# Four buffers instead of two for the expert weights, with the scratch of the dynamic DMAs halved

## The chip, the cores and the metric

The kernel runs on one core of a Trainium2 chip. The time is that of the device, in microseconds (us), from one run of the whole program; lower is better. Three runs of the kernel before gave 1428.39, 1423.75 and 1426.98 us, with a median of 1426.98 us.

## What is computed

Three stages follow each other. An attention between a sequence and a small state gives 8 x 544 = 4352 rows of 512 values. Each row is then sent to the one of eight experts whose embedding is nearest, and goes through that expert's two matrices (512 x 1024 and 1024 x 512). At last all rows go through a dense two-layer network (512 x 2048 and 2048 x 512). Cut to what matters, the reference is this:

```python
# attention, for x (8,8,512,64) and state (8,8,32,64)
a  = softmax(x @ state.T / 8);   xread = a  @ state
a2 = softmax(state @ x.T / 8);   sread = a2 @ x
x = concatenate([xread, sread], axis=2)          # then 4352 rows of 512
# experts
logits = normalise(x) @ normalise(expert_emb).T / tau
expert_idx = argmax(logits, axis=1)
gate_w = softmax(logits)[arange(N), expert_idx]
for e in range(8):
    mask = expert_idx == e
    h = maximum(x[mask] @ w1[e], 0.0)
    out[mask] = gate_w[mask, None] * (h @ w2[e])
# dense network
h = out @ w_in
g = h * clip(h + 3.0, 0.0, 6.0) / 6.0
result = g @ w_out
```

## The kernel before

**Stages.** The attention writes its rows to a table in DRAM (`xd`). The rows are sorted by expert into slots of 128 rows. The first five slots belong to the largest expert and form the lead: four of them are worked on together (`QUAD`) and one beside them (`FIFTH`), with the same weights. Behind them come 11 units of two slots and ten units of one slot (`RUN`); a few more units stand in branches at the end, for other distributions of the rows. The finished rows of a slot are stored to a second table in DRAM (`ysd`). The dense network takes blocks of 256 rows from that table, 17 of them (`Y`, `F1`, `F2`), and its matmuls are interleaved with those of the expert units as soon as the rows are there.

**Products in three parts.** Every matrix is split into a high part in the fp32r format and a low part, which is the rest. A product is three matmuls: high by high, low by high and high by low.

**The weights of an expert.** `load_w` (line 1236) loads 512 KB, 128 partitions x 2 x 512 values, into a buffer called `raw`, by a DMA that SP issues: line 1244 for the first matrix and line 1247 for the second. One unit takes four loads of each, and all units together take 176. A load is two pieces of 128 x 512 values. For each piece the high part `wh` is written by ACT or DVE (line 1258) and the low part `wl` by DVE or POOL (line 1261); the `raw` buffer is free again when both of its pieces have been split. The tiles `wh` and `wl` come from a pool of `NW = 3` pieces, and a piece is free when TensorE has used it. The first matrix is multiplied in `L1w` (line 1420, result `h_ps`), the second in `L2` (line 1523, result `y_ps`).

**The dense weights.** The dense matrices are 64-bit in DRAM. `Conv` (lines 267 to 326) loads them in 512 KB parts through ACT's queue, rebuilds the 32-bit values in several operations of ACT and DVE, and splits them into `wih`, `wil`, `woh` and `wol`. This takes place while the lead and the first units run.

**The rows of the dense network.** `Y` (line 1576) loads the rows of a block (`yl`, line 1590) through SP's queue, behind the stores to `ysd`. DVE transposes them, and ACT and DVE split them into `yh` and `yw`. `F1` (line 1629, result `u_ps`) and `F2` (line 1664, result `o`) are the matmuls.

**The order of the work.** Nothing is scheduled on the chip: each engine runs its instructions in the order in which the program emits them. That order comes from a planner in the kernel, the class `Sched`. Every piece of work has a cost on each engine that may do it, a due time, dependencies and buffers. The planner keeps one `Ring` for each kind of buffer, with the times at which its buffers come free. It then picks again and again the work with the smallest sum of possible start and weighted due time, so the sizes of the rings shape the order of all queues. The line that makes the rings is

```python
    NRAW, NW, NROW, NGX = 2, 3, 5, 4
    RG = {n: Ring(k) for n, k in dict(... raw=NRAW, w=NW, wraw=NRAW, ...).items()}
```

and the pool of the real buffers is opened with the same number, when the attention's memory has been given back:

```python
        pools(mctx, (("raw", dict(bufs=NRAW)), ("wp", dict(bufs=NW)), ...
```

**Memory.** The scratch at the bottom of the on-chip memory holds the descriptors of the DMAs that POOL issues (the gathers `xg` and `xq` from `xd`, the stores to `ysd` and the scattered stores of the result). By default it takes 16 KB of each partition. The constants and the dense weights lie above it, then the pools named above, `raw` first.

Of the kernel before, what the change touches and what calls it, by code (L numbers as in the profile page):

```python
# [154 lines left out]
def kernel(  # L155
# [12 lines left out]
    nc = tc.nc  # L168
# [74 lines left out]
    copy = {"A": ACT.copy, "D": DVE.tensor_copy}  # L243


    NRAW, NW, NROW, NGX = 2, 3, 5, 4
    NAX, NXT, NSC, NE2, NE1, NA2, NAH, NXR = (3, 3, 1, 1, 2, 1, 1, 1)
    NHX = 4
    RG = {n: Ring(k) for n, k in dict(
# [1633 lines left out]
```

## Time and profile before

| | |
|---|---|
| median of three runs | 1426.98 us (1423.75 to 1428.39) |
| the profiled execution's own time | 1424.93 us |
| its span | 1423.3 us |
| matmuls on TensorE (PE) busy | 1337.1 us, 94% of the span |
| VectorE (DVE) busy | 871.8 us, 61% |
| ScalarE (ACT) busy | 608.6 us, 43% |
| GpSimd (POOL) busy | 410.6 us, 29% |
| mean granted TensorE clock | 0.961 of full speed |

The span is what the hardware profiler saw of the program's instructions; the execution's own time is 1.6 us longer. PE is TensorE's matmuls, PEld its weight loads, SP the engine that only issues DMAs; a q behind a name (SPq, ACTq, POOLq) is the queue of that engine. A wait is written in square brackets: idle time before an instruction, and what ended it. A granted clock of 0.5 is 1.2 GHz and one of 1.0 is 2.4 GHz.

### The profile page before, as it was taken

The numbers are of one execution on the slowest core, as the hardware profiler recorded it, in microseconds if no ns is written. First come the engines' busy times: TensorE is split into PE (matmuls) and PEld (weight loads), VectorE is DVE, ScalarE is ACT, GpSimd is POOL, SyncE is SP. The second block draws the span as 40 slices with busy tenths as digits, with TensorE's granted clock in tenths as the row PEclk, the third lists the DMA queues.
The fourth block names the chain that finished last, engine by engine and source line by source line (L and its number), as shares of the span: only waits on it lengthen the run. The fifth ranks groups of instructions, "written<-read, shape, count | busy, mean of one in ns | idle before, by whom it ended". The sixth has DMA issues, their size and how long they took to land. (4 is left out here: it accounts for less than half of the span.)

```text
span 1423.3 us, 25424 instructions
## 1 busy us (share of the span) xinstructions
PE 1337.1 (94%) x9176; PEld 1189.1 (84%) x9176; DVE 871.8 (61%) x2047; ACT 608.6 (43%) x1318; POOL 410.6 (29%) x430
## 2 busy tenths in 40 slices
PE   7885797988899999999999999999999999999997
PEld 5664676877789889888989899998989999899996
DVE  5777966787566464656555446677776776334432
ACT  4885536676434333332424333343444443323332
POOL 3332545523432232233214223333223211100000
PEclk8996788989999999999999999999999999999999
DMA  7654347566563332333333233455454544101000
GB/s 175 182 167 168 107 135 195 172 192 204 153 190 97 112 99 97 113 104 106 112 100 118 90 105 124 163 154 165 150 164 149 164 141 151 46 15 30 16 16 16
DMA packets 151828, 176.48 MB, mean 124 GB/s; under 512 B 43856, under 2 KB 116560, under 8 KB 150672
## 3 DMA queue, kind: packets, MB, share of 16 engines
q1 hardware_dynamic: 128608, 121.47, 27.8%
q0 software_dynamic: 12336, 36.55, 8.1%
q10 hardware_dynamic: 10752, 16.78, 3.7%
q8 instruction: 73, 1.20, 0.4%
q14 instruction: 59, 0.48, 0.1%
HBM read 146.65 MB, written 28.10 MB: 123 GB/s over the span
## 5 line engine op out<-in xcount | busy, mean ns | idle before, releaser
L1629 PE MATMUL u_ps<-yh,wih 128*128 128x256 f32 x1088 | 308.3, 283 | 4.8 <-ACT yh L1605 3.7
L1629 PE MATMUL u_ps<-yw,wih 128*128 128x256 f32 x1088 | 308.2, 283 | 0.3 <-DVE yw L1608 0.3
L1629 PE MATMUL u_ps<-yh,wil 128*128 128x256 f32 x1088 | 307.9, 283 | 0.0
L1633 ACT ACTIVATE r<-u_ps,three 128x256 f32<-128x256 f32 x272 | 129.3, 475 | 356.7 <-PE u_ps L1629 337.2
L1636 DVE SCALAR_TENSOR_TENSOR u_ps<-r,u_ps 128x256 f32<-128x256 f32 x272 | 116.4, 428 | 232.3 <-ACT r L1633 219.7
L1629 PEld LDWEIGHTS u_ps<-yh,wih 128*128 128x128 f32 x1088 | 206.9, 190 | 14.3 <-ACT yh L1605 3.9
L1664 PE MATMUL o<-woh,gh 128*128 128x512 f32 x544 | 216.2, 397 | 0.8 <-DVE yo L1678 0.6
L1664 PE MATMUL o<-wol,gh 128*128 128x512 f32 x544 | 215.9, 397 | 0.0
L1664 PE MATMUL o<-woh,gl 128*128 128x512 f32 x544 | 215.1, 395 | 0.0
L1629 PEld LDWEIGHTS u_ps<-yw,wih 128*128 128x128 f32 x1088 | 206.8, 190 | 9.0 <-DVE yw L1608 0.5
L1629 PEld LDWEIGHTS u_ps<-yh,wil 128*128 128x128 f32 x1088 | 207.6, 191 | 0.0
L1261 DVE TENSOR_TENSOR wl<-raw,wh 128x512 fp32r<-128x512 f32 x280 | 195.8, 709 | 7.1 <-ACT wh L1258 2.3
L1640 ACT CAST gh<-u_ps 128x256 fp32r<-128x256 f32 x272 | 101.5, 373 | 206.7 <-PE o L1664 170.6
L1643 DVE TENSOR_TENSOR gl<-u_ps,gh 128x256 fp32r<-128x256 f32 x272 | 115.0, 423 | 114.3 <-ACT gh L1640 104.1
L1523 PE MATMUL y_ps<-wh,hx 128*128 128x512 f32 x512 | 184.9, 398 | 0.0
L1261 POOL TENSOR_TENSOR wl<-raw,wh 128x512 fp32r<-128x512 f32 x72 | 101.8, 1415 | 232.8 <-DVE wh L1258 125.7
L1289 POOL DMA_INDIRECT xq<-xd,qidx x128 | 130.9, 1023 | 59.0 <-issue 32.3
L1420 PE MATMUL h_ps<-xt,wh 128*128 128x256 f32 x704 | 141.0, 289 | 0.0
L1258 DVE CAST wh<-raw 128x512 fp32r<-128x512 f32 x226 | 101.2, 450 | 51.1 <-PE y_ps L1523 20.5
L1683 POOL DMA_INDIRECT out_dram<-yo,ix x34 | 38.0, 1118 | 301.4 <-DVE yo L1678 203.1
L1664 PEld LDWEIGHTS o<-woh,gl 128*128 128x128 f32 x544 | 102.4, 188 | 24.2
L1420 PE MATMUL h_ps<-xt,wl 128*128 128x256 f32 x352 | 103.0, 293 | 17.8 <-DVE wl L1261 11.9
(297 smaller groups left out, 2230.4 us busy)
## 6 DMA issues: line engine op xcount, KB each, us to landing
raw<-in_moe_w_dram SPq DMA_DIRECT2D x176, 512.0 KB
xd<-xr SPq DMA_DIRECT2D x8, 1088.0 KB
yl<-ysd SPq DMA_DIRECT2D x136, 64.0 KB
ysd<-yt POOLq DMA_DIRECT2D x32, 256.5 KB
xb<-in_x_dram SPq DMA_DIRECT2D x48, 128.0 KB
yw<-in_moe_w_out_dram ACTq DMA_DIRECT2D x9, 512.0 KB
cv_raw<-in_moe_w_in_dram ACTq DMA_DIRECT2D x8, 512.0 KB
yh<-in_moe_w_in_dram ACTq DMA_DIRECT2D x8, 512.0 KB
```

What stands on the lines that cost most here:

```text
L1258: copy[e](pc["hi"], box["t"][:, j, :])
L1261: eng[e].tensor_tensor(pc["lo"], box["t"][:, j, :], f32(pc["hi"]), op=ALU.subtract)
L1289: POOL.indirect_dma_start(q[:, j * QW:(j + 1) * QW], None, xd_q, index(qidx[:, j, s:s + 1]))
L1420: PE.matmul(out(f), pc[w][:, (2 * c + f) * 128:(2 * c + f + 1) * 128], u.xt[a][:, 2 * j + c, 256 * hf:256 * hf + 256], start=new and c == ...
L1523: PE.matmul(u.y[i], u.ht[t][:, a, lo + 128 * i:lo + 128 * i + 128], pc[w], start=c == 0 and k == 0, stop=c == KF - 1 and k == 2)
L1629: PE.matmul(p, w, y[:, k, :], start=k == 0 and j == 0, stop=k == KD - 1 and j == 2)
L1633: ACT.activation(q["r"], q["p"], AF.Relu, bias=pool["three"][:, 0:1], scale=unit_i)
L1636: DVE.scalar_tensor_tensor(q["p"], q["r"], 6.0, q["p"], op0=ALU.min, op1=ALU.mult)
L1640: ACT.copy(q["h"], q["p"])
L1643: DVE.tensor_tensor(q["l"], q["p"], f32(q["h"]), op=ALU.subtract)
L1664: PE.matmul(o["o"][a], g[:, a * 128:(a + 1) * 128], w, start=m == 0 and j == 0, stop=m == KFF - 1 and j == 2)
L1683: POOL.indirect_dma_start(out, bass.IndirectOffsetOnAxis(ap=o["ix"][:, a:a + 1], axis=0), box["t"], None)
```

## The change

The number of `raw` buffers goes from two to four, in the pool and in the planner's rings `raw` and `wraw` alike. Each buffer takes 4 KB of a partition, so 8 KB more are needed. The scratch of the dynamic DMAs is made 8 KB instead of 16 KB. The pools from `wp` upwards therefore keep their addresses, and what lies below `raw` moves down by 8 KB.

```diff
-    NRAW, NW, NROW, NGX = 2, 3, 5, 4
+    NRAW, NW, NROW, NGX = 4, 3, 5, 4
...
-    nc = _bacc.Bacc("TRN2", target_bir_lowering=False, num_devices=1)
+    nc = _bacc.Bacc("TRN2", target_bir_lowering=False, num_devices=1,
+                    dynamic_dma_scratch_size=8192)
```

## Rows read from the trace of the kernel before

**Rows 1.** The page: busy time of each engine, and the chain's shares.
```profile
PE 1337.1 (94%) x9176; PEld 1189.1 (84%) x9176; DVE 871.8 (61%) x2047; ACT 608.6 (43%) x1318; POOL 410.6 (29%) x430
...
PE 14%; DMA 0%; POOLq 0%; issue 0%; ACT 0%
```

**Rows 2.** Busy times of two stretches: PE, PEld, DVE, ACT, POOL, granted clock, DMA share, GB/s.
```profile
200.00:400.00 200.00, 172.55 (x967) 151.17 (x967) 143.21 (x327) 114.38 (x237) 86.72 (x83) 0.91 0.60 184
400.00:1220.00 820.00, 819.18 (x5223) 739.10 (x5223) 508.60 (x1172) 318.54 (x729) 240.40 (x233) 1.00 0.41 127
```

**Rows 3.** Waits of PE from 200 to 400 us: total, times, longest.
```profile
PE h_ps L1420 <- DVE wl L1261: 11.9, 7, 5.4
...
PE y_ps L1523 <- DVE wl L1261: 5.6, 4, 2.4
PE u_ps L1629 <- ACT yh L1605: 3.7, 1, 3.7
```

**Rows 4.** Waits for and by the loads, 137 to 420 us: SP, DVE, ACT.
```profile
SPq L1247 <- DVE wl L1261: 83.6, 16, 15.4
...
DVE wh L1258 <- DMA raw<-in_moe_w_dram: 1.9, 3, 0.9
...
ACT wh L1258 <- DMA raw<-in_moe_w_dram: 4.0, 4, 1.8
```

**Rows 5.** Timeline of SP's queue: start, duration, instruction, count.
```profile
213.94 9.96 SPq L1244 DMA_DIRECT2D raw<-in_moe_w_dram  x2
...
228.48 0.40 SPq L1244 DMA_DIRECT2D raw<-in_moe_w_dram  x1
...
235.92 6.72 SPq L1590 DMA_DIRECT2D yl<-ysd  x8
242.91 0.41 SPq L1244 DMA_DIRECT2D raw<-in_moe_w_dram  x1
```

**Rows 6.** Timeline of PE and ACT around the first dense block.
```profile
247.02 0.38 PE L1629 MATMUL u_ps<-yh,wih 128*128 128x256 f32 x1 [3.69 <-ACT yh L1605]
...
248.00 1.64 ACT L1258 CAST wh<-raw 128x512 fp32r<-128x512 f32 x3
...
253.06 0.39 PE L1420 MATMUL h_ps<-xt,wl 128*128 128x256 f32 x1 [0.76 <-DVE wl L1261]
```

**Rows 7.** Busy times of shorter stretches, columns as in rows 2.
```profile
137.00:147.00 10.00, 2.27 (x24) 1.78 (x22) 8.17 (x30) 4.04 (x8) 6.80 (x7) 0.50 0.77 259
...
236.00:243.00 7.00, 7.00 (x43) 7.00 (x43) 2.16 (x4) 1.81 (x3) 2.49 (x3) 0.66 1.08 250
...
247.00:253.00 6.00, 4.94 (x25) 4.53 (x25) 5.96 (x7) 3.74 (x7) 4.74 (x4) 0.72 0.25 76
...
300.00:345.00 45.00, 36.35 (x198) 31.68 (x199) 39.95 (x85) 33.62 (x65) 9.90 (x9) 0.89 0.62 206
```

**Rows 8.** The chain that ended last: one of its pieces.
```profile
1224.85 1.44 PE u_ps L1629 x12
```

**Rows 9.** Timeline of a later gap: load, split, matmul.
```profile
289.94 1.72 SPq L1244 DMA_DIRECT2D raw<-in_moe_w_dram  x2
...
302.82 0.68 DVE L1261 TENSOR_TENSOR wl<-raw,wh 128x512 fp32r<-128x512 f32 x1
...
303.56 0.58 PE L1420 MATMUL h_ps<-xt,wl 128*128 128x256 f32 x1 [3.64 <-DVE wl L1261]
```

**Rows 10.** Timeline of the longest gap.
```profile
386.93 0.56 POOL L1554 DMA_DIRECT2D ysd<-yt  x1 [5.12 <-DMA ysd<-yt]
...
389.71 0.58 PE L1420 MATMUL h_ps<-xt,wl 128*128 128x256 f32 x1 [5.42 <-DVE wl L1261]
```

**Rows 11.** Timeline of the lead's start.
```profile
151.59 1.97 PE L1314 MATMUL m_g<-ident,xp 128*128 128x128 f32 x8 [1.20 <-ACT xp L1309]
...
156.89 1.28 DVE L1320 TENSOR_TENSOR x<-m_g,x 128x512 fp32r<-128x512 f32 x2
```

**Rows 12.** The page's group of POOL's gathers.
```profile
L1289 POOL DMA_INDIRECT xq<-xd,qidx x128 | 130.9, 1023 | 59.0 <-issue 32.3
```

## The prediction, made before the changed kernel ran

> **What bounds the kernel now.** I read the page first. TensorE's matmuls are busy for 1337.1 of 1423.3 us, and the chain that ended last, as far as it is followed back, is made of matmuls [rows 1]. Next I cut the span into stretches. From 400 to 1220 us PE is busy for 819.18 of 820 us at full clock [rows 2], and behind that only the dense network is left. Nothing that comes sooner to SBUF can shorten that part: it ends earlier only if it starts earlier. What is to be had lies before 400 us. From 200 to 400 us PE is busy for 172.55 of 200 us, so it stands for 27.45 us, and the granted clock of 0.91 costs another 15.5 us (172.55 x 0.09): 43 us lost in all [rows 2].
>
> The third view says what PE waits for in that stretch: 11.9 us for low parts of first-matrix pieces, 5.6 us for those of the second matrix, and 3.7 us once, for the rows of the first dense block [rows 3]. So weights are named most often, and the question is whether they are late because their load was late. The fourth view answers in two halves. SP stands before its loads nearly all the time, 83.6 us before those of the second matrix alone, until a low part has been written and a buffer is free [rows 4]: the ring of two is always full. But the engines that split the weights hardly ever wait for a load: DVE 1.9 us and ACT 4.0 us, with a longest wait of 1.8 us [rows 4]. A full ring is no late load. So each gap has to be looked at by itself, and this is the step on which the forecast rests.
>
> **What the gaps show.** At 303.56 us PE has waited 3.64 us for a low part that DVE began at 302.82 us. The loads of this unit were issued from 289.94 us on, 13 us earlier [rows 9]. The weights were there and DVE was doing other work that the planner had put first: from 300 to 345 us it is busy for 39.95 of 45 us [rows 7]. The longest gap, 5.42 us, is a chain through POOL: a store waits 5.12 us for an earlier store, and what stands behind it in the queues holds up DVE [rows 10]. Neither is a matter of buffers.
>
> One place is. The first pair of slots needs four first-matrix loads. The first three are issued from 213.94 to 228.48 us. The fourth comes at 242.91 us, behind the eight loads of the dense rows, which began at 235.92 us and took SP 6.72 us [rows 5]. PE finishes pieces 0 to 5, stands 3.69 us until the dense rows are there at 247.02 us, and then, when it returns to piece 6, stands 0.76 us more for its low part at 253.06 us, since ACT could begin the split only at 248.00 us [rows 6]. With four buffers the fourth load finds a free buffer two loads earlier, that is before the eight loads rather than behind them. Pieces 6 and 7 can then be ready while PE stands.
>
> **The change part by part.**
>
> *The two buffers, at this place.* Two pieces are 24 matmuls, 2.88 us at full clock by the piece of the chain with twelve such matmuls in 1.44 us [rows 8]. They move into the 3.69 us in which PE stands: −2.9 us. The wait before piece 6 goes with them: −0.8 us. After the gap PE ran 4.94 us at a clock of 0.72, which costs 1.4 us [rows 7]. With most of the gap filled I take 1.0 us of that back (between 0, if what is left of the gap still lowers the clock, and 1.4). The room to split two pieces sooner is there: from 236 to 243 us DVE is busy for 2.16 and ACT for 1.81 of 7 us [rows 7]. `NW` stays at three, so piece 6 can be split as soon as piece 3 has been used, which is in this stretch. If that cover were gone the two pieces would come at 248 us as now, and the gain would be nothing.
>
> *The two buffers, elsewhere.* Loads land sooner for the few splits that did wait for one. That is bounded by 0 and by the 5.9 us of these waits [rows 4]. Most of them are not on PE's path, so I take −0.8 us.
>
> *The order.* The larger rings let the planner pick loads earlier, and every queue behind them may be shuffled: SP's (stores to `ysd`, rows of the dense network), DVE's, ACT's, POOL's and PE's. The loads are the same 512 KB each, only two ahead, so in the long run the traffic of any stretch is the same. The cost of the shuffle isn't in the trace; I take 0 and keep both ends: a gain up to what remains of the waits for weights, and a loss as large as four pieces of splitting in a stretch where DVE is full (both below, as rivals).
>
> *The scratch.* Halved, it might make POOL wait for room for descriptors. A gather takes 1.02 us to issue, and the idle time before all 128 is 59.0 us, of which 32.3 us has no releaser [rows 12]; gathers stand well apart. POOL is busy for 29% [rows 1], which would cover some more. I take 0. If the cover failed, the price is that of the one POOL chain that did reach PE, 5.42 us [rows 10].
>
> *The move of the memory by 8 KB* changes no instruction: 0. What lay under the two new buffers is attention data, whose work is over when the loads start.
>
> The sum is −2.9 − 0.8 − 1.0 − 0.8 = −5.5 us. Against the profiled execution's own 1424.93 us that is 1419.4 us. That execution is 2.05 us below the median of the three runs, so against 1426.98 us it is 1421.5 us, and this is what I predict.
>
> A rule speaks for more. The Trainium skill (Perfetto Trace Analysis, Optimization Strategy) says that the same gap repeating on the engine that should be saturated can mean too little SBUF for the next tile, by the count of buffers. By that rule the 17.5 us of waits for low parts would go; the trace agrees that the ring is full, but not that the loads are late.
>
> **The rivals.**
>
> *More goes than one gap.* The planner, believing loads earlier, also splits the other pieces earlier. The waits for low parts are 17.5 us [rows 3]; less the POOL chain (5.42) and the gap with DVE full (3.64) 8.4 us are left. Each microsecond stood has cost 0.56 us of clock on top (15.5 / 27.45), so 13.1 us; with the 4.7 us of the forecast that lie outside these waits the time is 1409 us. For it: the ring is always full. Against it: `NW` holds splitting to three pieces ahead whatever has landed, and the splitters waited only 5.9 us for loads. The skill's rule above would come out here.
>
> *Hidden.* The planner leaves the first dense block where it is in PE's order, pieces 6 and 7 wait behind it, and the 3.69 us stand: 1427 us, give or take the shuffle. For it: that gap is ended by dense rows, not weights.
>
> *Slower by the order.* With four more pieces in SBUF the planner splits them sooner, at 300 to 345 us, where DVE is at 39.95 of 45 us, and the dense weights that DVE converts there come later. Four pieces take 4.9 us (0.55 us for a high part, three in 1.64 us [rows 6], and 0.68 us for a low part [rows 9]). If PE stands for all of it and loses clock at 0.56, that is +7.7 us: 1434.7 us. It decides from the point at which DVE has no idle time left, some 5 us in those 45. Against it: three pieces stay the limit.
>
> *Slower at the lead's start.* Four loads instead of two go out at 137 us beside the gathers of the lead's rows: 1.05 MB more at 259 GB/s [rows 7] is 4.0 us. The transposes of these rows end at 153.56 us, and DVE turns to them at 156.89 us [rows 11], so 3.3 us are covered and 0.7 us is left, or all 4.0 us if the planner notices and reorders: 1428 to 1431 us. The Trainium skill (DMA: Bandwidth & Descriptors, Issuing engines are not separate DMA queues) says that DMAs of all issuing engines share the same 16 DMA engines and interleave. By it the gathers would be slowed by the loads; the DMA share of 0.77 in that stretch leaves some room, and no run here yet shows the collision.
>
> **How the numbers follow.** The forecast has 0.40, more gaps 0.15, hidden 0.25, slower by the order 0.13, slower at the start 0.07. A change of 0.3%, 4.3 us, is about what a measurement of this kernel can tell from none, so faster is below 1422.7 us and slower above 1431.3 us. The forecast lies only 1.2 us inside: of its 0.40 I put 0.28 with faster and 0.12 with no change. Hidden is no change; the rival at the start is mostly that (0.05). This gives 0.43 faster, 0.42 no change and 0.15 slower. The range must reach into the rivals on both sides: down to 1409 us, where more gaps go, and up to 1434 us, where the order costs. The forecast's own range is 1417 to 1427 us, from all of its terms at their better ends to none.
>
> **What would show it.** In the profile after: the fourth first-matrix load of the first pair issued before the eight loads of dense rows, and two more pieces of `h_ps` before the first `u_ps`; SP's waits for buffers as long as now, since a ring that is always ahead stays full; the gaps near 303 and 390 us still there, in one form or another; the stretch from 400 us on the same and only earlier. I am wrong if the first dense block still comes after six pieces, if the gaps for low parts vanish together, or if new waits for dense weights appear at `u_ps` and `o`.

## The result, and the profile of the changed kernel

The changed kernel takes 1408.42 us, the median of six runs (1407.13 to 1413.59), where the kernel before, run beside it, takes 1425.61 us. The ratio is 0.9896, with a 95% interval of 0.9877 to 0.9914. The forecast was 1421.5 us in a range of 1409 to 1434 us: the sign is right, and the time lies 0.6 us below the range. As the experiments show, it comes from two things, of which the forecast had only one: about half is the buffers and the order planned for them, with shorter waits of PE, and about half is matmuls that run faster because two tiles moved by 96 bytes.

The page of the changed kernel, beside [rows 1]: PE is busy 11.2 us less, and the chain has the same form.

```profile
PE 1325.9 (94%) x9176; PEld 1176.0 (84%) x9176; DVE 875.6 (62%) x2069; ACT 595.7 (42%) x1296; POOL 406.8 (29%) x430
...
PE 14%; DMA 0%; POOLq 0%; issue 0%; ACT 0%
```

Its busy times by stretch, columns as in [rows 2]:

```profile
200.00:400.00 200.00, 178.85 (x1024) 154.91 (x1023) 153.36 (x353) 117.82 (x246) 84.14 (x82) 0.94 0.65 198
400.00:1220.00 820.00, 816.35 (x5244) 735.93 (x5243) 508.11 (x1175) 306.10 (x708) 241.58 (x235) 1.00 0.41 124
260.00:400.00 140.00, 128.72 (x763) 111.47 (x762) 119.88 (x264) 85.89 (x179) 48.82 (x49) 0.96 0.68 209
```

From 200 to 400 us PE is busy for 6.3 us more, at a clock of 0.94 rather than 0.91. The third row is the part in which most of it happens; the same stretch before was

```profile
260.00:400.00 140.00, 120.48 (x697) 105.94 (x696) 101.33 (x229) 79.84 (x163) 51.07 (x50) 0.91 0.58 182
```

so PE is busy there for 8.2 us more, and the clock costs 128.72 x 0.04 = 5.1 us rather than 120.48 x 0.09 = 10.8 us. The waits of PE from 200 to 400 us, beside [rows 3]:

```profile
PE h_ps L1420 <- DVE wl L1261: 10.2, 6, 4.1
PE u_ps L1629 <- ACT yh L1605: 4.9, 1, 4.9
PE y_ps L1523 <- DVE wl L1261: 1.9, 2, 1.4
PE u_ps L1629 <- DVE gl L1643: 1.9, 1, 1.9
```

Waits for low parts fell from 17.5 to 12.1 us. They became small rather than vanished. The wait for the rows of the first dense block is 4.9 us instead of 3.7, but no growth is shown by this: three more kernels with the order and the two buffers of before (`place_8k`, `place_96` and `place_both`, below) stand 5.8 to 7.0 us there. The waits for and by the loads, beside [rows 4]:

```profile
SPq L1247 <- DVE wl L1261: 70.3, 13, 11.2
...
ACT wh L1258 <- DMA raw<-in_moe_w_dram: 0.9, 1, 0.9
```

The ring of four is still nearly always full: SP stands before loads of the second matrix for 70.3 us instead of 83.6. The engines that split waited 5.9 us for loads and now wait 0.9 us; DVE has no such wait left.

**The first dense block.** SP's queue, beside [rows 5], and the first matmul of the block, beside [rows 6]:

```profile
226.70 0.40 SPq L1247 DMA_DIRECT2D raw<-in_moe_w_dram  x1
227.43 8.80 SPq L1551 DMA_DIRECT2D ysd<-yt  x3
236.42 0.40 SPq L1247 DMA_DIRECT2D raw<-in_moe_w_dram  x1
...
237.48 9.04 SPq L1590 DMA_DIRECT2D yl<-ysd  x8
246.79 1.04 SPq L1247 DMA_DIRECT2D raw<-in_moe_w_dram  x2
```

```profile
250.26 0.58 PE L1629 MATMUL u_ps<-yh,wih 128*128 128x256 f32 x1 [4.91 <-ACT yh L1605]
```

All first-matrix loads of the pair are out before the dense rows; what goes ahead of them now are second-matrix loads (line 1247). PE has done pieces 0 to 7 when it stops, not 0 to 5. But the dense rows come later: the block begins at 250.26 us instead of 247.02, and PE stands 4.91 us instead of 3.69.

One execution of each kernel can't show how much of this is the change, since the first matmul of the pair begins anywhere from 227.1 to 230.8 us in the kernels of this document. Counted from there, the loads of the dense rows begin 7.2 to 8.0 us later in the five kernels with the order of before and 9.0 to 10.2 us later in the eight with the new order and four real buffers. The block begins 18.3 to 21.5 us later in the five, and 21.9 to 23.2 in the eight, which do 24 matmuls more ahead of it. In the trace of the kernel before it came earlier than in any other.

**The later gaps.** Near the gap of [rows 9] PE stands 1.01 us instead of 3.64; it has then done 24 more matmuls of this pair. The two stores of [rows 10] still stand 5 us apart, but earlier against PE's work, and where PE stood 5.42 us it now stands 0.74, 36 matmuls further on:

```profile
303.21 0.39 PE L1420 MATMUL h_ps<-xt,wl 128*128 128x256 f32 x1 [1.01 <-DVE wl L1261]
```

```profile
373.52 0.61 POOL L1554 DMA_DIRECT2D ysd<-yt  x1
378.57 0.56 POOL L1554 DMA_DIRECT2D ysd<-yt  x1 [4.44 <-ACT gh L1640]
...
382.96 0.38 PE L1420 MATMUL h_ps<-xt,wl 128*128 128x256 f32 x1 [0.74 <-DVE wl L1261]
```

**Behind 400 us.** The first matmul of the fifth pair of slots (line 1420) begins at 406.74 us, before it was 419.87: 13.1 us are won there. The end comes 17 us earlier, so another 4 us are won where PE hardly ever stops. The chain that ended last shows how. Where [rows 8] has twelve matmuls of `u_ps` in 1.44 us, the changed kernel has

```profile
1366.50 1.37 PE u_ps L1629 x12
1367.87 1.40 PE o L1664 x6
1369.27 1.37 PE u_ps L1629 x12
1370.64 1.41 PE o L1664 x6
1372.05 1.44 PE u_ps L1629 x12
```

Within one block the group of twelve takes 1.37 us up to chunk 7 and 1.44 us from chunk 8 on. Chunks 0 to 7 have their weights in `wih` and `wil`, chunks 8 to 15 in `wih2` and `wil2`. The mean duration of such a matmul, 282 ns in the page, doesn't show this, since matmuls overlap: the distance of their starts does.

What moved: `wih` and `wil` lie 8 KB lower, as the diff says. `yh` and `yw`, the moving rows, lie 96 bytes higher. Their pool lays out its tiles in the order of their first use. Before, the conversion of the dense weights used `yw` and `yh` first; in the new order the three index tiles `ix` of the dense rows (32 bytes each) come first.

### The profile page after: what moved, and what is told of

It is laid out like the page before. It is cut to its first block, busy times and chain, and to the rows that moved or that the text cites. A ratio compares the mean times of both kernels' runs of the same rounds, so it can differ in the third digit from the quotient of the medians.

```text
span 1406.5 us, 25411 instructions
## 1 busy us (share of the span) xinstructions
PE 1325.9 (94%) x9176; PEld 1176.0 (84%) x9176; DVE 875.6 (62%) x2069; ACT 595.7 (42%) x1296; POOL 406.8 (29%) x430
## 5 line engine op out<-in xcount | busy, mean ns | idle before, releaser
L1629 PEld LDWEIGHTS u_ps<-yh,wih 128*128 128x128 f32 x1088 | 206.5, 190 | 17.5 <-ACT yh L1605 5.1
L1289 POOL DMA_INDIRECT xq<-xd,qidx x128 | 130.6, 1020 | 55.1 <-issue 34.6
L1420 PE MATMUL h_ps<-xt,wh 128*128 128x256 f32 x704 | 137.2, 284 | 0.0
L1258 DVE CAST wh<-raw 128x512 fp32r<-128x512 f32 x245 | 106.9, 437 | 44.2 <-PE y_ps L1523 21.9
L1664 PEld LDWEIGHTS o<-woh,gh 128*128 128x128 f32 x544 | 102.2, 188 | 18.2 <-ACT yo L1680 1.7
```

The source lines that it names most:

```text
L1258: copy[e](pc["hi"], box["t"][:, j, :])
L1289: POOL.indirect_dma_start(q[:, j * QW:(j + 1) * QW], None, xd_q, index(qidx[:, j, s:s + 1]))
L1420: PE.matmul(out(f), pc[w][:, (2 * c + f) * 128:(2 * c + f + 1) * 128], u.xt[a][:, 2 * j + c, 256 * hf:256 * hf + 256], start=new and c == ...
L1629: PE.matmul(p, w, y[:, k, :], start=k == 0 and j == 0, stop=k == KD - 1 and j == 2)
L1664: PE.matmul(o["o"][a], g[:, a * 128:(a + 1) * 128], w, start=m == 0 and j == 0, stop=m == KFF - 1 and j == 2)
```

## The experiments

Each time is a median; the ratio is to the kernel before, run beside it (1424 to 1426 us). Added pools move line numbers by a few. The edits are shown against the changed kernel, that of experiment 2 against the kernel before; `...` marks code left out.

**1. The 8 KB and the scratch alone** (`place_8k`): old order, two buffers, 8 KB left unused behind them.

```diff
-    NRAW, NW, NROW, NGX = 4, 3, 5, 4
+    NRAW, NW, NROW, NGX = 2, 3, 5, 4
...
-        pools(mctx, (("raw", dict(bufs=NRAW)), ("wp", dict(bufs=NW)), ...
+        pools(mctx, (("raw", dict(bufs=NRAW)), ("pad", dict(bufs=1)), ("wp", dict(bufs=NW)), ...
...
+        DVE.memset(pool["pad"].tile([128, 2048], F32, name="pad")[:, 0:1], 0.0)
```

> The order and the two load buffers of before; only the const pool, the first half of the dense in-weights and the load buffers lie 8 KB lower, as after the change (scratch halved, 8 KB left unused behind the load buffers). If the 8 KB are what makes the matmuls of L1629 for the chunks below 8 start every 115 rather than 119.8 ns: 1632 matmuls x 4.6 ns = 7.5 us less, about 1418 us against 1425.6, and 115/119.8 ns in the trace. If the faster matmuls belong to the new order, or to the 96 bytes by which yh and yw moved: no change, 1424 to 1427 us, 119.8 ns everywhere. If halving the scratch costs anything by itself, it shows here as more than 1427 us.

1424.96 us, ratio 1.0005 (0.9991 to 1.0019); groups of `u_ps` take 1.44 us as before. Neither half the scratch nor the move by 8 KB costs or gains anything beyond 0.2%.

**2. The 96 bytes alone** (`place_96`): kernel before, with 96 unused bytes ahead of the pool of `yh` and `yw`. `gh` and `gl` behind them move by 96 too.

```diff
-                     ... ("wob", dict(bufs=1)), ("ffn", dict(bufs=1))))
+                     ... ("wob", dict(bufs=1)), ("pad96", dict(bufs=1)), ("ffn", dict(bufs=1))))
+        DVE.memset(pool["pad96"].tile([128, 24], F32, name="pad96")[:, 0:1], 0.0)
```

> The order, the two load buffers and the scratch of before; only yh and yw (and what lies above them) lie 96 bytes higher, as after the change. If the 96 bytes make the matmuls of L1629 for the chunks below 8 faster: about 1418 us and 115 ns there. If the 8 KB or the order do it: no change, 1424 to 1427 us, 119.8 ns everywhere.

1413.22 us, ratio 0.9920 (0.9897 to 0.9942): an unused 96 bytes give 11 us, more than expected. The chain, where a block begins:

```profile
1360.08 1.37 PE o L1665 x6
1361.45 1.37 PE u_ps L1630 x12
1362.82 1.38 PE o L1665 x6
```

The groups of `u_ps` in the first half take 1.37 us, and, unforeseen, those of `o` 1.38 instead of 1.40: there `gh` and `gl` are the weights, and they had moved too.

**3. Both moves** (`place_both`): old order, both additions above.

> The order and the two load buffers of before with both moves of memory, 8 KB down for the first half of the dense in-weights and 96 bytes up for yh and yw. Theory 'placement and order share the gain': 1418 to 1420 us, 115 ns for the chunks below 8 and 120 ns for the others, the waits up to 420 us as before. Rival 'all of it is the order and the buffers': 1424 to 1427 us. Rival 'all of it is placement': 1408 to 1410 us.

1415.82 us, ratio 0.9934 (0.9912 to 0.9955), the same as with the 96 bytes alone, within the intervals; 1.37 us in the first half and 1.43 in the second. The first theory holds in kind; the time lies 2 us below its range, and groups of `o` are faster here too (1.38 us).

**4. The new order at the old places** (`new_order_old_place`): two of the four buffers lie in the 8 KB taken from the scratch, `ix` behind the pool of `yh` and `yw`.

```diff
+    raw_low = ctx.enter_context(tc.tile_pool(name="raw_low", bufs=2, reuse_waits="tile"))
     const = ctx.enter_context(tc.tile_pool(name="const", bufs=1))
...
-            t = box["t"] = pool["raw"].tile( ...
+            n_raw[0] += 1
+            t = box["t"] = (pool["raw"] if n_raw[0] % 2 else raw_low).tile( ...
...
-                    o["ix"] = pool["ffn"].tile( ...
+                    o["ix"] = pool["ixp"].tile( ...
```

> Four load buffers and the order planned for them, but two of the buffers lie in the 8 KB taken from the scratch, so that the dense weights, yh and yw keep the addresses of before. Theory 'placement and order share the gain': the milestones up to 420 us come 11 to 13 us earlier as after the change, the matmuls of L1629 start every 119.8 ns, and the time is 1413 to 1417 us. Rival 'all of it is the order and the buffers': 1408 us and 115 ns. Rival 'all of it is placement': 1424 to 1427 us.

1413.66 us, ratio 0.9924 (0.9900 to 0.9947), `u_ps` at 1.43 us in both halves. The new order gains without the 96 bytes. The fifth pair of slots begins at 411.52 us, 8.4 us earlier than before and not 11 to 13. It is not quite clean: `gh` and `gl` lie 96 bytes lower here, and groups of `o` take 1.39 us. Experiment 5 mends that.

**5. The changed kernel without the 96 bytes** (`after_y_first`): `yh` and `yw` get a pool of their own below `ix`, and every tile of the dense network but `wih` and `wil` lies where it lay before.

```diff
-                     ... ("wob", dict(bufs=1)), ("ffn", dict(bufs=1))))
+                     ... ("wob", dict(bufs=1)), ("ffy", dict(bufs=1)), ("ffn", dict(bufs=1))))
...
-                    o["y"] = [pool["ffn"].tile([128, KD, 256], F32R, tag=x, name=x, bufs=2) for x in ("yh", "yw")]
+                    o["y"] = [pool["ffy"].tile([128, KD, 256], F32R, tag=x, name=x, bufs=2) for x in ("yh", "yw")]
```

> The kernel after, with yh and yw in a pool of their own below the three index tiles ix, so that they, r, gh and gl lie where they lay before the change; nothing else moves. Theory 'the 96 bytes are about 6 us of the gain': 1414 to 1416 us, L1629 every 119.6 ns in both halves, the stretch up to 420 us as after. Rival 'the 96 bytes and the new order don't add up': 1408 us in spite of 119.6 ns.

1416.11 us, ratio 0.9941 (0.9927 to 0.9956). This is what buffers and order are worth: 8 us. The rest is the 96 bytes: 1416.11 - 1408.42 = 7.7 us (8.3 us between the spans, 1414.8 and 1406.5; 6.4 us by the two ratios, 0.9941 and 0.9896, each of which has its own runs of the kernel before). The chain says the same: 136 groups (17 blocks of 8 chunks) times 0.06 to 0.07 us are 8 to 9.5 us. The border between two blocks shows no step:

```profile
1357.68 1.44 PE u_ps L1629 x12
1359.12 1.39 PE o L1664 x6
1360.52 1.44 PE u_ps L1629 x12
```

The fifth pair of slots begins 10.4 us earlier than before:

```profile
409.44 0.28 PE L1420 MATMUL h_ps<-xt,wh 128*128 128x256 f32 x1
```

So buffers and order win 10.4 us up to there and lose some 2 us of them again: 8.5 us are left between the spans (1423.3 and 1414.8). By the distances of PE's starts most of the loss lies between 1000 and 1050 us, where PE waits 1.2 us for a low part that POOL writes.

**6. Four real buffers, old order** (`four_real_old_order`): four buffers in the pool, two in the planner's rings.

```diff
-    NRAW, NW, NROW, NGX = 4, 3, 5, 4
+    NRAW, NW, NROW, NGX = 2, 3, 5, 4
...
-        pools(mctx, (("raw", dict(bufs=NRAW)), ("wp", dict(bufs=NW)), ...
+        pools(mctx, (("raw", dict(bufs=4)), ("wp", dict(bufs=NW)), ...
```

> Four load buffers in SBUF and the smaller scratch, but the order of before on every engine: the planner still counts two. The fourth first-matrix load stays behind the eight loads of the dense rows. Theory 'the buffers gain only through the order planned for them': 1422 to 1426 us, SP's waits for buffers shorter, PE's waits up to 420 us as before. Rival 'the loads themselves were late': the waits of PE for low parts shrink without a new order, 1415 to 1420 us.

1421.24 us, ratio 0.9969 (0.9957 to 0.9981), between the two theories: the time is that of the first, but PE's waits up to 420 us did shrink, from 11.9 to 7.0 us for first-matrix low parts. Most of it is the longest gap. With the order of before on every engine it is

```profile
374.28 1.77 SPq L1590 DMA_DIRECT2D yl<-ysd  x4
...
379.89 0.60 POOL L1554 DMA_DIRECT2D ysd<-yt  x1 [2.37 <-ACT yt L1543]
385.17 0.56 POOL L1554 DMA_DIRECT2D ysd<-yt  x1 [4.68 <-ACT hx L1439]
...
387.95 0.38 PE L1420 MATMUL h_ps<-xt,wl 128*128 128x256 f32 x1 [2.06 <-DVE wl L1261]
```

Before, SP sent these four loads of dense rows later, behind weight loads that had waited for a buffer, and POOL's first store came later too:

```profile
375.51 1.86 SPq L1590 DMA_DIRECT2D yl<-ysd  x4
...
381.21 0.60 POOL L1554 DMA_DIRECT2D ysd<-yt  x1 [5.70 <-DVE wl L1261]
```

The store follows some 5.6 us behind the rows in both kernels. That it waits for them is argued from this equal distance, since the profile names other releasers. PE reaches the place 1.6 us later than before and stands 2.06 us instead of 5.42: the gap ends 1.8 us earlier, and the rest by which it is shorter is PE's later arrival. The gap at 303 us is shorter too, 2.64 us, but only for that reason: it ends at 305.68 us, 2.1 us later than before, with the same work ahead of it on DVE.

**7. The new order with three real buffers** (`new_order_3_real`): experiment 5, with one buffer taken away and its 4 KB left unused.

```diff
-        pools(mctx, (("raw", dict(bufs=NRAW)), ("wp", dict(bufs=NW)), ...
+        pools(mctx, (("raw", dict(bufs=3)), ("pad", dict(bufs=1)), ("wp", dict(bufs=NW)), ...
```

> The same, and only three of the four load buffers are real, while every engine keeps the order planned for four. Theory 'the order carries what is left of the gain, the loads are early enough with fewer buffers': within 2 us of the same kernel with four, 1414 to 1417 us. Rival 'the loads themselves must be two further ahead': SP's queue stands longer, the dense rows behind the loads come later, 1418 us or more.

1426.44 us, ratio 1.0011 (1.0001 to 1.0021): the gain is gone, and the first theory fell. SP's queue, three of its waits, and the first dense matmul:

```profile
237.20 0.40 SPq L1248 DMA_DIRECT2D raw<-in_moe_w_dram  x1
...
239.37 0.68 SPq L1248 DMA_DIRECT2D raw<-in_moe_w_dram  x1
...
244.22 11.42 SPq L1591 DMA_DIRECT2D yl<-ysd  x8
```

```profile
SPq L1248 <- DVE gates L1369: 10.1, 1, 10.1
SPq L1591 <- DMA yw<-in_moe_w_out_dram: 5.9, 1, 5.9
SPq L1591 <- DMA ysd<-yt: 2.9, 1, 2.9
```

```profile
258.50 0.58 PE L1630 MATMUL u_ps<-yh,wih 128*128 128x256 f32 x1 [12.29 <-ACT yh L1606]
```

The load for which the fourth buffer is missing waits 10.1 us, and the lead's last stores and the dense rows wait behind it in SP's queue. The row loads then wait another 11 us of their own, which the profile puts down to loads of dense weights (5.9 and 2.2 us) and to the stores (2.9); no run takes these apart. PE stands 12.29 us at the first dense block, in experiment 5 6.0. PE's wait for a low part just before the block is 4.7 us, in the changed kernel 4.1: what is late isn't the weights but what is queued behind their load. Against experiment 5 some 7 us are lost by 400 us, and 3 us more behind 850 us, where PE waits once 1.6 and once 1.4 us for ACT.

**8. Is it a copy that holds back the first dense block?** (`early_copy`): the changed kernel, with DVE's copy of row indices into the lead's last `yt` ahead of the gate work.

```diff
                           ... AF.Copy, scale=o["ga"])
+            if u is FIFTH:
+                DVE.tensor_copy(o["yt"][:, DM:YW].bitcast(I32), oidx[:, s:s + 1])
         def yb():
-            DVE.tensor_copy(o["yt"][:, DM:YW].bitcast(I32), oidx[:, s:s + 1])
+            if u is not FIFTH:
+                DVE.tensor_copy(o["yt"][:, DM:YW].bitcast(I32), oidx[:, s:s + 1])
```

> The kernel after, with one instruction moved on DVE: the copy of the row indices into the lead's last yt (0.14 us) stands ahead of two gate normalisations and a low part, about 2 us earlier. Theory 'the first dense block is late because this copy holds back the lead's last store, and with it SP's loads of the dense rows': the store is issued at 233.6 rather than 235.8 us, the first u_ps comes 2 us earlier than the 250.3 us of after, and the gap before it falls from 4.9 to about 3 us; 2 us less, 1405 to 1407 us, which the trace will show better than the time. Rival 'the load of 512 KB that the new order puts ahead of the dense rows holds them back': the gap stays at 4.9 us and the time at 1408 us.

1408.78 us, ratio 0.9881 (0.9859 to 0.9903): no change of the time. The copy comes at 234.37 instead of 235.69 us, and the three stores end 1.3 us earlier, but the load behind them still comes at 236.53 and the rows at 237.55:

```profile
228.76 6.14 SPq L1554 DMA_DIRECT2D ysd<-yt  x3
236.53 0.40 SPq L1247 DMA_DIRECT2D raw<-in_moe_w_dram  x1
...
237.55 9.49 SPq L1593 DMA_DIRECT2D yl<-ysd  x8
```

In this execution all is 1.3 us later from the start: the pair's first matmul begins at 228.60 us, in the changed kernel at 227.27. Counted from there the stores end 2.7 us earlier, but the load and the rows begin only 1.2 to 1.3 us earlier and the first `u_ps` 0.65. SP now waits 1.7 us at that load, and PE stands 5.67 us. So the theory fell: half of what the copy gives up is taken by the wait at the load, and PE's wait isn't shorter at all. The rival fits, and experiment 7 speaks for it. That the load's 512 KB also slow the rows isn't shown: the eight row loads take 9.04 us in the changed kernel and 6.72 before, but 8.9 to 10.4 us in `place_8k`, `place_96` and `place_both`, which have the order of before.

**9 to 12. What the 96 bytes do.** Four kernels with the change, its order and its buffers, and unused bytes between the pools. `y_at_32` and `y_at_64` have 64 and 96 bytes ahead of the pool of `yh` and `yw`. `aligned_all` has 32 bytes ahead of `wih2`, 96 ahead of `woh2` and 32 ahead of `gh`. `best` has 160, 96 and 96 there, and in the expert part 160 ahead of `xt` and 96 ahead of `hx`. The edit of `aligned_all`:

```diff
-        pools(mctx, (("wib", dict(bufs=1)), ("py", dict(bufs=1, space=PSUM)), ("pu", dict(bufs=2, space=PSUM)),
-                     ("po", dict(bufs=1, space=PSUM)), ("wob", dict(bufs=1)), ("ffn", dict(bufs=1))))
+        pools(mctx, (("pad1", dict(bufs=1)), ("wib", dict(bufs=1)), ("py", dict(bufs=1, space=PSUM)), ("pu", dict(bufs=2, space=PSUM)),
+                     ("po", dict(bufs=1, space=PSUM)), ("pad2", dict(bufs=1)), ("wob", dict(bufs=1)), ("ffn", dict(bufs=1)), ("pad4", dict(bufs=1)), ("ffg", dict(bufs=1))))
+        DVE.memset(pool["pad1"].tile([128, 8], F32, name="pad1")[:, 0:1], 0.0)
+        DVE.memset(pool["pad2"].tile([128, 24], F32, name="pad2")[:, 0:1], 0.0)
+        DVE.memset(pool["pad4"].tile([128, 8], F32, name="pad4")[:, 0:1], 0.0)
...
-            q["h"], q["l"] = (pool["ffn"].tile( ...
+            q["h"], q["l"] = (pool["ffg"].tile( ...
```

> The kernel after, with wih2 and wil2 moved by 32 bytes, so that they stand to yh and yw as wih and wil do (32 against 96 in units of 128 bytes), and gh and gl moved to a multiple of 128. Theory 'the start of weights and moving rows within 128 bytes sets the pace of the matmul': L1629 starts every 114 to 115 ns in both halves and L1664 every 231 ns, so 1632 x 5 ns + 1632 x 2.5 ns = 12 us less, about 1396 us. Rival 'only the first half's region can be fast': as after, 1408 us, at best 1404 by gh and gl.

1403.62 us, ratio 0.9853 (0.9833 to 0.9874). Neither the theory nor its rival: the second half went to 1.36 us, `o` to 1.39, but the first half, in which in units of 128 bytes nothing had changed, went from 1.37 to 1.41:

```profile
1366.27 1.41 PE u_ps L1632 x12
1367.68 1.39 PE o L1667 x6
...
1377.45 1.36 PE u_ps L1632 x12
```

> The kernel after with yh, yw and what lies above them 96 bytes higher, so that yh and yw begin at 64 in units of 128 bytes. Theory 'a difference of 64 bytes between weights and moving rows is the fast one': now the second half (weights at 0) runs at 114 to 115 ns and the first (at 32) at 120. Rival 'only 32 or 0 within 64 bytes counts, and 0 is slow': both halves at 120 ns, about 1414 us. Rival 'any move away from 0 is fast for the first half': 115 in the first half, 1408 us.

1402.31 us, ratio 0.9837 (0.9811 to 0.9863): 1.40 us in the first half, 1.39 in the second. Half right: the second became faster, though not as fast as 1.36 or 1.37, and the first didn't go back to 1.44.

> The kernel after with yh, yw and what lies above them 64 bytes higher, so that yh and yw begin at 32 in units of 128 bytes. Theory 'a difference of 64 bytes is the fast one': both halves at 120 ns, about 1415 us. Rival 'only 32 or 0 within 64 bytes counts': as after, first half 115, second 120, 1408 us.

1415.81 us, ratio 0.9933 (0.9909 to 0.9957). The time is that of the first theory, but the halves differ, 1.44 us in the first and 1.41 in the second:

```profile
1354.35 1.41 PE u_ps L1630 x12
1355.76 1.40 PE o L1665 x6
1357.16 1.44 PE u_ps L1630 x12
```

Put in units of 256 bytes, all of these fall into one order, with some overlap. The table has the start of the moving rows minus the start of the weights, modulo 256, by the addresses of the built programs, and the time of a group in the chain's last block:

| kernel | `u_ps`, first half | `u_ps`, second half | `o` |
|---|---|---|---|
| before, `place_8k`, `after_y_first` | 96: 1.44 us | 0: 1.44 us | 160: 1.40 us |
| after | 192: 1.37 | 96: 1.44 | 160: 1.40 to 1.41 |
| `place_96`, `place_both` | 192: 1.37 | 96: 1.43 | 64: 1.38 |
| `new_order_old_place` | 96: 1.43 | 0: 1.43 | 0: 1.39 |
| `aligned_all` | 64: 1.41 | 192: 1.36, at its start 1.39 to 1.42 | 0 and 128: 1.39 |
| `y_at_64` | 32: 1.40 | 192: 1.39 | 64: 1.37 to 1.39 |
| `y_at_32` | 0: 1.44 | 160: 1.41 | 96: 1.39 to 1.40 |

In every kernel that has 192 it goes with the faster half of `u_ps`, and 64 goes with the fastest `o`. The difference doesn't fix the time by itself: 192 gave 1.36 to 1.37 us with the weights at 32 or 160 modulo 256 (up to 1.42 where the half begins in `aligned_all`), but 1.39 with them at 128 (`y_at_64`), so the place itself may count too; and in `y_at_64` `o` took 1.37 us in one half and 1.39 in the other at the same difference. `best` was built from this table alone, with 192 in both halves and in the pairs' `h_ps` as well, and 64 for `o`:

> The kernel after, with unused bytes between the pools so that moving rows minus weights, taken in units of 256 bytes, is 192 for both halves of L1629 (wih and wih2 alike) and for L1420 of the pairs (xt against wh), and 64 for L1664. Theory 'this difference sets the pace of the matmul': 115 ns in both halves of L1629, 115 ns in L1420, 231 ns in L1664: 1632 x 4.6 + 1632 x 3 + 1536 x 2.4 ns = 16 us less than after, 1392 us. Rival 'the pace goes by the absolute address or by the units of 128': one of the three stays as it was, 1396 to 1404 us.

1392.69 us, ratio 0.9786 (0.9768 to 0.9804): 15.7 us less than the changed kernel, where 16 had been worked out. Its chain, with no step in the dense stretch:

```profile
1334.61 1.37 PE u_ps L1634 x12
1335.97 1.38 PE o L1669 x6
1337.36 1.36 PE u_ps L1634 x12
```

Nine steps from start to start of the pairs' `h_ps` take 1.02 us (from 491.12 to 492.14 us), where the changed kernel takes 1.05 (489.74 to 490.79). It is the fastest of all, 31 us under the kernel before, and its step beyond the changed kernel costs only unused bytes.

## Why the prediction was right, and where it was not

**The sum.** The forecast had -5.5 us for buffers and order, and nothing for places in memory. Experiment 5 measures the first at -8.4 us (0.59% of 1424) and experiment 5 against the changed kernel the second at -6.4 to -7.7 us. The sign of the first was right and its size a third too small; the place and the reasons of the gain were mostly others than forecast, so that the nearness is in part luck.

**What failed first: "*The move of the memory by 8 KB* changes no instruction: 0".** As written it holds (experiment 1). But the change moved more than the text saw: through the new order it moved `yh` and `yw` by 96 bytes, and that is half of the result. The busy share of 819.18 in 820 us [rows 2] was read as a bound that only an earlier start could move. It says that PE never stops, not that it runs as fast as it can. The Trainium skill (SBUF — State Buffer, SBUF: two separate sides) says that on the engines' side only the port pair of VectorE and GpSimd causes contention and that PE never waits on anyone. It speaks of engines against each other and names no cost of a place; by it alone one would have expected some 1416 us instead of 1408.42. Here groups took 1.36 to 1.44 us by place alone, and the measurement decides; whether that is a wait at the memory at all no run here shows.

**"*The two buffers, at this place*", -2.9 - 0.8 - 1.0.** The step happened and the gain didn't. Pieces 6 and 7 stand before the first dense block, and the wait of 0.76 us is gone. But the block began 3.2 us later. Counting a matmul of 256 columns as 0.118 us and one of 512 as 0.234, the work that the kernel before had done at 260 us was done only some 0.5 us earlier, and in experiment 5 1.5 us later. Counted from the pair's first matmul this work ends after 31.1 to 33.4 us with the two buffers and the order of before (four kernels), and after 31.9 to 33.0 us with four buffers and the new order (eight kernels). The clock from 247 to 253 us was 0.58 instead of 0.72, but `place_8k` and `place_both`, with the order of before, have 0.50 and 0.54. The error lies in the word "behind": the text had the loads overtake the dense rows and didn't ask what the dense rows then wait for, although it is one queue (experiments 7 and 8). The 3.69 us on which it rested were the shortest such wait of all the traces.

**"Neither is a matter of buffers".** This is the step that failed in the forecast of the waits. With four buffers and the order of before the gap at 390 us ends 1.8 us earlier, so it was a matter of buffers; the gap at 303 us ends 2.1 us later, so it was not (experiment 6). With the new order as well, PE stands 0.74 us instead of 5.42 near the one and 1.01 us instead of 3.64 near the other. The gain of buffers and order was made between 300 and 400 us, where the forecast had next to nothing: by the same counting of matmuls, and counted from the pair's first matmul, the eight kernels with four buffers and the new order are about level with the four at 300 us (69.3 to 72.9 us against 69.8 to 71.2) and 8 to 13 us ahead at 400 us (158.6 to 162.2 us against 170.6 to 171.3). From 260 to 400 us all of PE's waits are 18.9 to 19.9 us in the four and 11.1 to 14.8 us in the eight, and the granted clock is 0.91 to 0.93 and 0.96 to 1.00. In the changed kernel waits for low parts and gates went from 19.5 to 8.0 us, in experiment 5 to 11.6, and new ones of 2.7 and 1.8 us came for `gl`. The argument was that a load issued 13 us before cannot be late. True, but a load that waits for its buffer holds up every other instruction behind it in SP's queue, stores and dense rows. That this reaches PE is shown at the first dense block (experiment 7); for the later gaps it is argued from experiment 6. The text also read SP's waits as longer than they are: those for low parts before loads of both matrices add up to 189.6 of 283 us, two thirds and not nearly all the time.

**"*The order* ... I take 0".** Too small. Buffers without the order give -4.4 us (0.31%), with it -8.4 us, and the order without the fourth buffer +1.6 us (0.11%). The order gains nothing without its buffers, and the buffers alone give half.

**"*The scratch* ... I take 0".** Right: 1.0005, and the gathers took 1020 ns each with 55.1 us of idle time before them [rows 12].

**The rivals.** *More gaps go* gave 1409 us, next to the 1408.42 measured, but this is luck: without the 96 bytes buffers and order brought 1416. The rule of the Trainium skill on repeated gaps (Perfetto Trace Analysis, Optimization Strategy) pointed the right way; 5.4 of the 17.5 us went in the changed kernel and 5.9 in experiment 5, not all. *Hidden* had the right outcome at the first dense block, no gain there, for another reason: pieces 6 and 7 did move ahead of it. *Slower by the order* didn't come about in the stretch named: PE is busy there for 39.17 us instead of 36.35, DVE for 38.61 instead of 39.95 [rows 7]. With three real buffers a small loss (0.11%) does come, in SP's queue and not on DVE. *Slower at the lead's start* is not seen: with the loads beside the gathers the stretch from 137 to 147 us carried 286 GB/s instead of 259, the last transposes began at 151.22 us instead of 151.59 [rows 11], and the lead's first matmul at 151.99 instead of 153.21.

**The tests named.** Two more pieces before the first `u_ps`: yes. A ring as full as before: nearly (SP's waits of 189.6 us are 168.5 now). Gaps near 303 and 390 still there: in a small form. "the stretch from 400 us on the same and only earlier": no, and this was the test that found the 96 bytes. None of the signs of being wrong came: the block stands behind eight pieces, gaps for low parts are left, and the new waits before `u_ps` and `o` are for `gl` and not for dense weights. They would not have shown where this forecast failed.

## What to carry to other kernels

Here a full ring cost PE through the instructions queued behind the waiting load (experiment 7) more than through the load's own data; before valuing another buffer, list what stands behind each waiting load and who waits for that. When an edit changes pools, sizes or the order of first use, compare the distance of starts of equal matmuls before and after, in a stretch without waits, before any gain is put down to waits. Before a gap of one trace is made a term of the sum, look at the same gap in a second execution: one of 3.69 us here was 5.8 to 7.0 us in three others. And where PE is busy all the time, try a few unused bytes between the tiles that it streams and those it loads as weights: 32 to 160 bytes were worth 16 us of 1408 here.

## What the runs showed of the hardware

The pace of fp32r matmuls depends on where moving rows and weights lie against each other. For 256 columns, twelve took 1.36 to 1.44 us at full clock, 113 to 120 ns each; for 512 columns six took 1.37 to 1.41 us, 228 to 235 ns each. The difference of the starts modulo 256 bytes puts the differences tried in order (0, 32, 64, 96, 160 and 192 for `u_ps`; 192 the fastest, mostly at 1.36 to 1.39 us, 0 and 96 the slowest at 1.43 to 1.44), and `best`, built from it, came out at the time worked out beforehand; it doesn't explain the spread at 192, in which the place of the weights may count. Units of 128 don't do it: `aligned_all` went from 1.37 to 1.41 us without a change in them. A move of `wih` and `wil` by 8 KB, which leaves the places modulo 256 as they are, had no effect. Which part of the chip makes this difference no run here shows. Halving the scratch of the dynamic DMAs cost nothing with 231 DMAs issued by POOL, 128 of them the gathers `xq` of [rows 12].
